# A block's attention in two unbroken stretches on TensorE, in place of up to six

## The chip, the cores and the metric

The kernel runs on one core of a Trainium2 chip. The metric is the device time of the whole program in microseconds (us). Times within the program come from one profiled execution, read by a hardware profiler.

## The reference

A linear attention with a complex decay for each channel runs over 768 tokens for 4 batches and 8 heads of 48 channels; its output goes through a two-layer network with a leaky ReLU.

```python
scale = np.minimum(mag, 0.999) / (mag + 1e-06)          # mag: of a_re + i a_im
for t in range(S):                                      # S = 768
    S_re, S_im = (ar*S_re - ai*S_im) + kv, ar*S_im + ai*S_re
    y[:, :, t] = np.einsum('bhd,bhde->bhe', q[:, :, t], S_re)
x = y.transpose(0, 2, 1, 3).reshape(3072, 384)
h = x @ w_in                                            # 384 -> 2048
return np.maximum(0.01 * h, h) @ w_out                  # 2048 -> 384
```

## The kernel before, in words

The 768 tokens of a batch are cut into six chunks of 128. A **block** is one chunk of one batch, all eight heads: 24 blocks. Two blocks make a **sub** `n` (0 to 11) and also a **group** `g` of 256 tokens for the network. (n, 0) and (n, 1) are the blocks of sub n. For each sub VectorE and ScalarE prepare decayed `q` and `k` (`prep`, L637: tiles `a`, `u`, `sq`, `xs`, `qk`, `qkt`), and twenty DMAs carry them from `qkt` into the layout by heads, `t96` (`relay_of`, L842; the trace writes `t`).

`attend` (L886) then does one block. On TensorE these are small matmuls of 32 columns of the array, and two sets of transposes of 128 columns:

- the **scores** of heads 0 to 3 and of heads 4 to 7, 16 matmuls each into a bank of PSUM; VectorE multiplies each half by the mask into `asb`;
- the **transposes** of `k` of heads 0 to 3 and 4 to 7, four each into a bank; ScalarE copies each to `kn`;
- the **output**, 32 matmuls (16 in the first chunk) of `asb` with `v` and of the state `rst` with `q`, into the bank `px`; ScalarE makes of it `x` rounded (`xh`), VectorE the rest (`xl`);
- the **update** of the state, 24 matmuls of `kn` with `v` into the bank `pu`; VectorE adds it to `rst`, ScalarE scales it eight times.

Blocks of the last chunk (subs 10 and 11) have neither transposes nor update. In the trace every small float32 matmul has two records, the transposes one to each. Attention has three PSUM banks (`att0` to `att2`, `NATT`, L33), handed out by `Banks` (L179).

`forward` (L1078) is the network on TensorE: for a group 16 pieces of `first` (`ph<-x`) and `second` (`po<-hid`), of 9, or of 6 wide matmuls of 256 columns, 288 wide matmuls in all; between them `hide` makes `hid` of `ph` (ScalarE `tg`, VectorE `tg`, ScalarE `hid`, VectorE `hid`).

The order on each engine is made by a planner when the program is built. `drive` (L218) keeps tasks; a task is a generator that stops with `yield "P"` (or `"V"`, `"A"`, `"S"`) ahead of its next instructions on that engine, with what it needs. The task that could start first goes on, and among those near it the one of the lowest rank: attention (`R_ATT`, -3) goes ahead of the network (`R_FF`, 1000). At each stop on TensorE the network can come in between. `Banks.done` says that a bank is free in the plan, and so at each stop `attend` asks for one. `PLACE` (L76) gives the places in a group's stream of the network from which on the blocks of the next sub may stand.

Of the kernel before, what the change touches and what calls it, by code (L numbers as in the profile page):

```python
# [7 lines left out]
F32 = mybir.dt.float32  # L8
# [5 lines left out]
AF = mybir.ActivationFunctionType  # L14
# [3 lines left out]
B, H, S, D = 4, 8, 768, 48  # L18
# [3 lines left out]
P = 128  # L22
C = 128
# [5 lines left out]
TI = 3  # L29
# [26 lines left out]
QKT, T96, X0, X1, V, A, KN, STG, ST, HID = (0, 1), (2, 3), 4, 5, 6, 7, 8, 9, 10, (11, 12, 13)  # L56
# [24 lines left out]
WSC = 2.0**20  # L81
# [3 lines left out]
def block_lane(h, x):  # L85
    return (x + h) % NB


def score_order():

    todo = [[(h, x) for h in range(NB) for x in range(NB) if block_lane(h, x) == q] for q in range(NB)]
    free = [0] * NB
    order = []
    while any(todo):
        q = min((f, q) for q, f in enumerate(free) if todo[q])[1]
        h, x = todo[q].pop(0)
        order.append((h, x))
        free[q] += NB - x
    return order


class Lane:


    def __init__(self, tc, engine, cost):
        self.tc, self.engine, self.cost = tc, engine, cost
        self.last, self.clock, self.log = None, 0.0, []
# [71 lines left out]
class Banks:  # L179
# [5 lines left out]
    @property  # L185
    def done(self):
        return bool(self.free)

    @property
    def end(self):  # L190
        return min(self.free)[0]

    def take(self):
        k = min(self.free)[1]
        self.free = [x for x in self.free if x[1] != k]
        return self.tiles[k]

    def give(self, tile, at):
        self.free.append((at, next(k for k, t in enumerate(self.tiles) if t is tile)))


class Task:
# [208 lines left out]
def body(ctx, tc, keep, a_in, qk_in, v_in, w_in, out):  # L411
# [3 lines left out]
    pp = ctx.enter_context(tc.tile_pool(name="pp", bufs=1))  # L415
# [14 lines left out]
    xacc = keep.tile([P, NT // C], F32, tag="xacc", name="xacc")  # L430
# [5 lines left out]
    pe, dve, act = Lane(tc, nc.tensor, pe_cost), Lane(tc, nc.vector, dve_cost), Lane(tc, nc.scalar, act_cost)  # L436
# [24 lines left out]
    banks = Banks(att)  # L461
# [43 lines left out]
    fetched_a, fetched_qk, fetched_v, prepared, moved_q, moved_k, attended, hidden, stored, checked = ({} for _ in range(10))  # L505
# [55 lines left out]
    def freed(*places):  # L561
        return [x for x, r in zip(converted, ROUND) if r in places]
# [310 lines left out]
    def from_block(t96, s, h, bi, x0, x1):  # L873
        t = t96[:, slot_of(s, h), bi, 0:C].rearrange("p (y x) -> p y x", x=NB)
        return t[:, :, x0] if x1 == x0 + 1 else t[:, :, x0:x1]
# [3 lines left out]
    def xgroup(u):  # L879
        g = u // NGU  # L880
        if g not in xg:
            x = pp.tile([P, 2, TI, GT], F32R, tag="x", name=f"x_{g}", bufs=2)
            xg[g] = [x[:, 0], x[:, 1]]
        return *xg[g], (u % NGU) * C

    def attend(n, bi):  # L886
        c, bs = SUBS[n]
        b = bs[bi]
        u = SUB_POS[n] // C + bi
        g = u // NGU  # L890
        carry = c < NCH - 1
        at = [[placed[n, 2 * bi + k]] if n > 1 else [] for k in range(2)]
        yield "P", moved_q[n], moved_k[n], banks, *at[0], *([over[u - 1]] if u else [masked])
        qkt, t96 = relay[n]
        am = []
        for hh in range(2):
            if hh:
                yield "+P", banks
            ps = banks.take()
            for h4, x in score_order():  # L900
                h = hh * 4 + h4
                q = block_lane(h4, x)
                mm(
                    ps[32 * q : 32 * q + 32, h4].rearrange("p (y x) -> p y x", x=NB)[:, :, x:],
                    lhsT=from_block(t96, 1, h, bi, x, x + 1),
                    rhs=from_block(t96, 0, h, bi, x, NB),
                    start=True,
                    stop=True,
                )
            yield "V"  # L910
            asb = pp.tile([P, 4, C], F32, tag="asb", name=f"asb_{n}_{bi}_{hh}", bufs=2)
            dve.tensor_tensor(out=asb, in0=ps, in1=mask, op=ALU.mult)
            am.append(asb)
            banks.give(ps, attended[u].end + 0.8)
        for hh in range(2 if carry else 0):
            yield "P" if hh else "+P", banks, *(at[1] if hh else []), *([] if u else freed(KN))
            if hh == 0:
                kn = pp.tile([P, H, 2, D], F32, tag="kn", name=f"kn_{n}_{bi}")
            pt = banks.take()
            for h4 in range(4):  # L920
                pe.transpose(
                    out=pt[:, h4, 0:96],
                    in_=t96[:, slot_of(1, hh * 4 + h4), bi, 0:C],
                    identity=ident[0:96, 0:96],
                )
            yield "A"
            act.copy(kn[:, hh * 4 : hh * 4 + 4].rearrange("p h l d -> p h (l d)"), pt[:, :, 0:96])
            banks.give(pt, attended[u].end + 0.6)

        yield "P", fetched_v[n], banks, *at[1], *(  # L930
            [summed[g - 2]] if g > 1 else freed((X0, X1)[g])
        )
        xh, xl, x0 = xgroup(u)
        v = raw_v[n]
        px = banks.take()
        lanes4 = [[] for _ in range(4)]
        for x in range(4 * TI):
            k, part = divmod(x, 3)
            for h, off in ([(2 * k, 0)], [(2 * k, 32), (2 * k + 1, 48)], [(2 * k + 1, 80)])[part]:
                cols = slice(k * PAIR + off, k * PAIR + off + 32)  # L940
                first = off != 48
                last = off != 32
                lanes4[x % 4].append((x // 4, v[:, bi, cols], am[h // 4][:, h % 4], first, last and c == 0))
                if c > 0:
                    lanes4[x % 4].append(
                        (x // 4, rst[:, b, k, off : off + 32], t96[:, slot_of(0, h), bi, 0:C], False, last)
                    )
        for step in zip(*lanes4):
            for q, (i, lhsT, rhs, first, last) in enumerate(step):
                mm(px[32 * q : 32 * q + 32, i], lhsT=lhsT, rhs=rhs, start=first, stop=last)  # L950
        yield "A"
        act.activation(
            xh[:, :, x0 : x0 + C], px[:, 0:TI], AF.Copy, scale=-WSC * WSC, accum_out=xacc[:, u : u + 1]
        )
        if carry:
            yield "+P", banks
            pu_bank = banks.take()
            pu = pu_bank.rearrange("p a b -> p (a b)")
            for h in range(H):
                o = VW + h * D  # L960
                for q in range(3):
                    mm(
                        pu[32 * q : 32 * q + 32, h * D : (h + 1) * D],
                        lhsT=kn[:, h].rearrange("p l d -> p (l d)")[:, 32 * q : 32 * q + 32],
                        rhs=v[:, bi, o : o + D],
                        start=True,
                        stop=True,
                    )
        over[u].set(attended[u].end + 1.0)
        yield "V"  # L970
        dve.scalar_tensor_tensor(
            out=xl[:, :, x0 : x0 + C], in0=px[:, 0:TI], scalar=-WSC * WSC, in1=xh[:, :, x0 : x0 + C].bitcast(F32),
            op0=ALU.mult, op1=ALU.subtract,
        )
        split[u].set(attended[u].end + 0.6)
        banks.give(px, attended[u].end + 0.6)
        if not carry:
            return
        new = pu[0:96, 0:DM].rearrange("p (k j e) -> p k j e", j=2, e=D)
        r0 = rst[:, b, 0, 0]  # L980
        r = bass.AP(r0.tensor, r0.offset, [list(r0.ap[0]), [PAIR, H // 2], [64, 2], [1, D]])
        if c > 0:
            yield "+V"
            dve.tensor_tensor(out=r, in0=new, in1=r, op=ALU.add)
            banks.give(pu_bank, attended[u].end + 0.6)
        yield "A"
        src = new if c == 0 else r
        for h0 in (0, 1, 6):
            hn = 2 if h0 == 6 else 3
            s0 = slot_of(1, h0)  # L990
            for x in range(hn):
                h = h0 + (x if h0 == 6 else 2 * x)
                act.activation(
                    r[:, h // 2, h % 2], src[:, h // 2, h % 2], AF.Copy, scale=t96[:, s0 + x, bi, C : C + 1]
                )
        if c == 0:
            banks.give(pu_bank, attended[u].end + 2.5)
# [106 lines left out]
    split, over = ([Mark() for _ in range(NT // C)] for _ in range(2))  # L1104
# [3 lines left out]
    masked = task(masks(), R_HID, end=4.5)  # L1108
# [101 lines left out]
```

## Time and profile before

| | us |
|---|---|
| median of three runs | 643.27 (642.04 to 644.84) |
| the profiled execution | 643.89 |
| its span, first to last instruction | 642.2 |
| TensorE busy | 602.5 (94%) |
| VectorE busy | 532.3 (83%) |
| ScalarE busy | 380.7 (59%) |

PE is TensorE, DVE VectorE, ACT ScalarE, SP the queue that issues the DMAs. The times of a matmul's end are modelled, since matmuls run into each other; so durations on TensorE are best taken from one start to the next. All lines of the trace that are recorded through the planner have the line L111; the tiles tell the instructions apart.

### The profile page before, as it was taken

The numbers are of one execution on the slowest core, as the hardware profiler recorded it, in microseconds if no ns is written. First come the engines' busy times: TensorE is split into PE (matmuls) and PEld (weight loads), VectorE is DVE, ScalarE is ACT, GpSimd is POOL, SyncE is SP. The second block draws the span as 40 slices with busy tenths as digits, with TensorE's granted clock in tenths as the row PEclk, the third lists the DMA queues.
The fourth block names the chain that finished last, engine by engine and source line by source line (L and its number), as shares of the span: only waits on it lengthen the run. The fifth ranks groups of instructions, "written<-read, shape, count | busy, mean of one in ns | idle before, by whom it ended". The sixth has DMA issues, their size and how long they took to land.

```text
span 642.2 us, 18140 instructions
## 1 busy us (share of the span) xinstructions
PE 602.5 (94%) x7714; PEld 554.4 (86%) x7714; DVE 532.3 (83%) x916; ACT 380.7 (59%) x838; POOL 10.3 (2%) x33
## 2 busy tenths in 40 slices
PE   4992899999979999999999999999999999999995
PEld 2451568999969999999999999999999999999994
DVE  6999899899899999998999999999898998342340
ACT  6975766475474574764755746636656637667631
POOL 2000100100000000000000000000000000000000
PEclk9995999999999999999999999999999999999998
DMA  8844621422423235045053153152260362877200
GB/s 344 317 137 123 239 79 51 150 80 78 123 80 98 102 96 169 17 131 146 4 150 128 31 138 111 61 150 69 85 175 21 102 200 85 255 214 269 99 1 30
DMA packets 30200, 79.25 MB, mean 123 GB/s; under 512 B 5120, under 2 KB 11264, under 8 KB 30112
## 3 DMA queue, kind: packets, MB, share of 16 engines
q1 hardware_dynamic: 29728, 77.23, 38.2%
q8 instruction: 62, 1.02, 0.6%
q0 software_dynamic: 384, 0.79, 0.5%
q14 instruction: 26, 0.21, 0.1%
HBM read 54.26 MB, written 4.72 MB: 92 GB/s over the span
## 4 chain that ended last, share of the span: by engine, by line
PE 67%; DVE 21%; DMA 3%; ACT 3%; issue 2%; SPq 1%; DVEq 0%; ACTq 0%
PE po L111 27%; PE ph L111 26%; PE att L111 13%; DVE qkt L111 4%; DVE a L111 4%; DMA a<-in_a_dram 3%; DVE u L111 3%; SPq L111 1%; DVE sq L111 1%; DVE hid L111 1%; DVE tg L111 1%; PE pd L111 1%; ACT sq L111 1%; DVE wcv L111 1%; DVE xs L111 1%
## 5 line engine op out<-in xcount | busy, mean ns | idle before, releaser
L111 PE MATMUL po<-hid,wout_hi 128*128 128x256 f32 x1152 | 231.1, 289 | 0.0
L111 PE MATMUL ph<-x,win_hi 128*128 128x256 f32 x1152 | 216.6, 286 | 3.7 <-DVE x L111 1.5
L111 PEld LDWEIGHTS po<-hid,wout_hi 128*128 128x128 f32 x1152 | 182.8, 188 | 7.0 <-issue 3.4
L111 PEld LDWEIGHTS ph<-x,win_hi 128*128 128x128 f32 x1152 | 178.8, 190 | 6.7 <-DVE x L111 2.0
L111 PE MATMUL ph<-x,win_lo 128*128 128x256 f32 x576 | 162.8, 283 | 0.0
L111 PE MATMUL po<-hid,wout_lo 128*128 128x256 f32 x576 | 142.9, 282 | 0.0
L111 PEld LDWEIGHTS ph<-x,win_lo 128*128 128x128 f32 x576 | 109.4, 190 | 0.0
L111 PEld LDWEIGHTS po<-hid,wout_lo 128*128 128x128 f32 x576 | 108.4, 188 | 0.0
L111 DVE TENSOR_TENSOR tg<-ph,tg 128x512 f32<-128x512 f32 x96 | 65.8, 686 | 39.1 <-ACT tg L111 38.6
L111 ACT ACTIVATE tg<-ph 128x512 f32<-128x512 f32 x96 | 56.9, 593 | 61.8 <-PE ph L111 61.5
L111 ACT CAST hid<-tg 128x512 fp32r<-128x512 f32 x96 | 59.1, 617 | 55.8 <-DVE tg L111 55.6
L111 DVE TENSOR_TENSOR hid<-tg,hid 128x512 fp32r<-128x512 f32 x96 | 65.8, 686 | 14.5 <-ACT hid L111 14.2
L111 DVE TENSOR_TENSOR u<-a 128x384 f32<-128x384 f32 x84 | 46.7, 556 | 3.1 <-ACT a L111 1.4
L111 DVE TENSOR_TENSOR qkt<-qk,a 128x768 f32<-128x768 f32 x48 | 44.7, 951 | 1.6 <-ACT qkt L111 1.6
L111 PE MATMUL att<-t 96*32 96x128 f32 (+3 forms) x1536 | 42.6, 253 | 2.7 <-DVE x L111 2.2
L111 DVE TENSOR_TENSOR asb<-att,mask 128x512 f32<-128x512 f32 x48 | 32.8, 689 | 13.2 <-PE att L111 12.7
L111 PEld LDWEIGHTS att<-t 96*32 96x32 f32 x1536 | 35.1, 144 | 9.4 <-DVE x L111 2.8
L111 PE MATMUL att<-asb,v 128*32 128x128 f32 x768 | 37.0, 275 | 1.2 <-DVE asb L111 0.9
L111 ACT ACTIVATE rst<-rst,t 96x48 f32<-96x48 f32 x128 | 30.7, 322 | 11.7 <-DVE rst L111 11.4
L111 ACT ACTIVATE wck<-wck 128x1152 f32<-128x1152 f32 (+1 forms) x22 | 27.7, 1259 | 9.0 <-DMA wck<-in_w_dram 8.8
L111 PE MATMUL att<-t,rst 96*32 96x128 f32 x640 | 32.3, 272 | 0.0
L111 DVE TENSOR_TENSOR a<-u 128x192 f32<-128x192 f32 x84 | 29.8, 354 | 1.5
(171 smaller groups left out, 767.7 us busy)
## 6 DMA issues: line engine op xcount, KB each, us to landing
t<-qkt SPq DMA_DIRECT2D x92, 145.1 KB, 3.3
wck<-in_w_dram SPq DMA_DIRECT2D x10, 1152.0 KB, 5.8
v<-in_v_dram SPq DMA_DIRECT2D x12, 832.0 KB, 5.9
a<-in_a_dram SPq DMA_DIRECT2D x12, 768.0 KB, 4.8
qk<-in_qk_dram SPq DMA_DIRECT2D x12, 768.0 KB, 6.5
out_dram<-ot SPq DMA_DIRECT2D x12, 384.0 KB, 5.5
t<-qkt SPq DMA_DIRECT2D x46, 64.5 KB, 3.0
stage_st<-in_w_dram SPq DMA_DIRECT2D x3, 768.0 KB, 9.5
```

The source lines that it names most:

```text
L111: x = getattr(self.engine, name)(*args, **kw)
```

## The change

For subs 1 to 11 (`once`) `attend` has two stops on TensorE instead of up to six. The first, taken when three banks are free in the plan (`banks.some(3)`), records both halves of the scores and the first transposes; the second, again with three free banks, records the second transposes, the output and the update. In the last chunk there are no transposes and update, and the stops ask for two banks and one. The masks stand together behind the first stretch on VectorE, and the first `kn` copy behind them on ScalarE. Sub 0 keeps its order. No instruction is added or taken away on any engine.

```diff
+    def some(self, n):
+        return Some(self, n)
+class Some:
+    def __init__(self, banks, n):
+        self.banks, self.n = banks, n
+    @property
+    def done(self):
+        return len(self.banks.free) >= self.n
+    @property
+    def end(self):
+        return sorted(self.banks.free)[self.n - 1][0]
...
-        yield "P", moved_q[n], moved_k[n], banks, *at[0], *([over[u - 1]] if u else [masked])
+        once = n > 0
+        yield "P", moved_q[n], moved_k[n], *at[0], *([over[u - 1]] if u else [masked]), (
+            banks.some((3 if carry else 2) if once else 1)
+        )
...
+        if once:
+            ps = [scores(0), scores(1)]
+            if carry:
+                kn = pp.tile([P, H, 2, D], F32, tag="kn", name=f"kn_{n}_{bi}")
+                pt = keys(0)
+            yield "V"
+            masked_out(0, ps[0])
+            yield "+V"
+            masked_out(1, ps[1])
+            if carry:
+                yield "+A"
+                natural(0, pt)
...
-        yield "P", fetched_v[n], banks, *at[1], *(
+        yield "P", fetched_v[n], banks.some((3 if carry else 1) if once else 1), *at[1], *(
             [summed[g - 2]] if g > 1 else freed((X0, X1)[g])
         )
+        if once and carry:
+            natural(1, keys(1))
...
+        if carry and once:
+            pu_bank, pu = update()
         yield "A"
         act.activation(
             xh[:, :, x0 : x0 + C], px[:, 0:TI], AF.Copy, scale=-WSC * WSC, accum_out=xacc[:, u : u + 1]
         )
-        if carry:
-            yield "+P", banks
+        if carry and not once:
+            yield "+P", banks
+            pu_bank, pu = update()
```

What it moves is shown at three places, all in block (7, 1). The first is on TensorE, at the end of the scores. `att_...<-t` are scores, `att_...<-ident,t` transposes, `po` and `ph` wide matmuls of the network. Before:

```order
L111 MATMUL att_103<-t_7_4816 32x32x2
L111 MATMUL att_103<-t_7_4816 32x32
L111 MATMUL po_0_4960<-hid_3_5031,wout_hi 128x256
L111 MATMUL po_0_4960<-hid_3_5031,wout_lo 128x256
L111 MATMUL po_1_4961<-hid_3_5031,wout_hi 128x256
L111 MATMUL po_1_4961<-hid_3_5031,wout_lo 128x256
L111 MATMUL po_2_4962<-hid_3_5031,wout_hi 128x256
L111 MATMUL po_2_4962<-hid_3_5031,wout_lo 128x256
L111 MATMUL att_102<-ident,t_7_4816 128x96 x4
```

After:

```order
L111 MATMUL att_103<-t_7_4835 32x32x2
L111 MATMUL att_103<-t_7_4835 32x32
L111 MATMUL att_101<-t_7_4835 32x128
L111 MATMUL att_101<-t_7_4835 32x32x3
...
L111 MATMUL att_101<-t_7_4835 32x32x2
L111 MATMUL att_101<-t_7_4835 32x32
L111 MATMUL att_102<-ident,t_7_4835 128x96 x4
L111 MATMUL po_0_4941<-hid_4_5062,wout_hi 128x256
```

The six wide matmuls ahead of the transposes are gone, and so are those between the halves: the second half (`att_101`) follows the first (`att_103`) and the transposes follow the second half.

The second place is on TensorE as well, from the output (`att<-asb,v` and `att<-t,rst`) to the update (`att<-v,kn`). Before:

```order
L111 MATMUL att_103<-asb_1_1_5301,v_4790 32x128 x4
L111 MATMUL att_103<-t_7_4816,rst 32x128 x4
L111 MATMUL po_0_4960<-hid_4_5128,wout_hi 128x256
L111 MATMUL po_0_4960<-hid_4_5128,wout_lo 128x256
L111 MATMUL po_1_4961<-hid_4_5128,wout_hi 128x256
L111 MATMUL po_1_4961<-hid_4_5128,wout_lo 128x256
L111 MATMUL po_2_4962<-hid_4_5128,wout_hi 128x256
L111 MATMUL po_2_4962<-hid_4_5128,wout_lo 128x256
L111 MATMUL att_102<-v_4790,kn_1_5303 32x48 x24
```

After:

```order
L111 MATMUL att_103<-ident,t_7_4835 128x96 x4
L111 MATMUL att_101<-asb_1_0_5334,v_4808 32x128 x4
...
L111 MATMUL att_101<-asb_1_1_5343,v_4808 32x128 x4
L111 MATMUL att_101<-t_7_4835,rst 32x128 x4
L111 MATMUL att_102<-v_4808,kn_1_5316 32x48 x24
L111 MATMUL ph_7_5353<-x_4499,win_hi 128x256 x2
```

Second transposes, output and update now stand in a row, with the network behind them.

The third place is VectorE, around the two masks (`asb`) of the block. Before:

```order
L111 TENSOR_TENSOR asb_1_0_5273<-att_101,mask 128x512
L111 TENSOR_TENSOR qkt_5130<-qk_5021,a_4321 128x6x128
L111 TENSOR_TENSOR asb_1_1_5301<-att_103,mask 128x512
L111 TENSOR_TENSOR tg_5_5275<-ph_5_5218,tg_5_5275 128x512
L111 TENSOR_TENSOR qkt_5130<-qk_5021,a_4321 128x6x128
```

After:

```order
L111 TENSOR_TENSOR qkt_5282<-a_4363 128x2x768
L111 TENSOR_TENSOR a_4363<-a_4363 128x1536
L111 TENSOR_TENSOR asb_1_0_5334<-att_103,mask 128x512
L111 TENSOR_TENSOR asb_1_1_5343<-att_101,mask 128x512
L111 TENSOR_TENSOR tg_6_5331<-ph_6_5251,tg_6_5331 128x512
```

The masks stand together, with two of the preparation's longest instructions ahead of them. Over the whole program the new order has, in all 18 full blocks of subs 1 to 9, 18 to 27 wide matmuls between the two stretches of a block, and 18 to 36 before the other block of the sub. In subs 5 to 9 the first block of a sub begins behind 189 wide matmuls of its group (138 to 162 before) and the second behind 234 (198 or 204 before).

## Rows read from the trace of the kernel before

**Rows 1.** The page, busy time of each engine.
```profile
PE 602.5 (94%) x7714; PEld 554.4 (86%) x7714; DVE 532.3 (83%) x916; ACT 380.7 (59%) x838; POOL 10.3 (2%) x33
```
**Rows 2.** Stretches: length, busy PE, PEld, DVE, ACT, POOL, PEclk, DMA share, GB/s.
```profile
104.00:233.26 129.26, 124.72 (x1790) 118.39 (x1788) 120.92 (x206) 74.53 (x177) 2.86 (x8) 0.99 0.31 94
233.26:509.61 276.35, 276.23 (x3942) 264.89 (x3937) 253.88 (x429) 163.51 (x387) 0.73 (x6) 1.00 0.35 101
...
233.26:279.21 45.95, 45.83 (x663) 44.07 (x658) 44.09 (x74) 30.02 (x73) 0.12 (x1) 1.00 0.39 119
```
**Rows 3.** Waits of TensorE from 100 us on: total us, times, longest.
```profile
PE ph L111 <- DVE x L111: 1.5, 1, 1.5
PE ph L111 <- ACT x L111: 1.1, 1, 1.1
```
**Rows 4.** TensorE in time, block (5, 1): start, length, instruction, count.
```profile
311.28 0.88 PE L111 MATMUL att<-t 96*32 96x128 f32 x32
312.09 0.98 PE L111 MATMUL po<-hid,wout_hi 128*128 128x256 f32 x6
312.91 0.49 PE L111 MATMUL att<-ident,t 96*128 96x96 f32 x4
313.19 0.49 PE L111 MATMUL ph<-x,win_hi 128*128 128x256 f32 x2
...
316.60 0.43 PE L111 MATMUL att<-asb,v 128*32 128x128 f32 x8
...
318.50 0.39 PE L111 MATMUL po<-hid,wout_hi 128*128 128x256 f32 x1
...
319.42 0.88 PE L111 MATMUL att<-v,kn 128*32 128x48 f32 x48
320.23 0.39 PE L111 MATMUL po<-hid,wout_hi 128*128 128x256 f32 x1
```
**Rows 5.** The chain that ended last, in time: start, length, what.
```profile
246.87 2.16 PE ph L111 x18
```
**Rows 6.** TensorE in time, block (4, 0).
```profile
254.71 1.52 PE L111 MATMUL att<-t 96*32 96x128 f32 x64
256.17 0.55 PE L111 MATMUL att<-ident,t 96*128 96x96 f32 x4
256.50 0.96 PE L111 MATMUL po<-hid,wout_hi 128*128 128x256 f32 x6
257.30 0.49 PE L111 MATMUL att<-ident,t 96*128 96x96 f32 x4
```
**Rows 7.** TensorE in time, block (2, 1): the output and the update.
```profile
184.41 0.43 PE L111 MATMUL att<-asb,v 128*32 128x128 f32 x8 [0.89 <-DVE asb L111]
...
186.19 0.86 PE L111 MATMUL att<-v,kn 128*32 128x48 f32 x48
```
**Rows 8.** VectorE in time, block (5, 1): in brackets idle time before, its releaser.
```profile
312.26 0.69 DVE L111 TENSOR_TENSOR asb<-att,mask 128x512 f32<-128x512 f32 x1 [0.18 <-PE att L111]
...
319.92 0.55 DVE L111 SCALAR_TENSOR_TENSOR x<-att,x 128x384 fp32r<-128x384 f32 x1
```
**Rows 9.** TensorE in time, block (2, 0): second scores, last of the output.
```profile
169.96 0.87 PE L111 MATMUL att<-t 96*32 96x128 f32 x32
...
175.51 0.41 PE L111 MATMUL att<-t,rst 96*32 96x128 f32 x8
```
**Rows 10.** VectorE in time, block (2, 0): second mask, and `x`.
```profile
173.19 0.68 DVE L111 TENSOR_TENSOR asb<-att,mask 128x512 f32<-128x512 f32 x1
...
180.48 0.55 DVE L111 SCALAR_TENSOR_TENSOR x<-att,x 128x384 fp32r<-128x384 f32 x1
```
**Rows 11.** The chain that ended last, up to the first wide matmuls of group 3.
```profile
209.18 4.69 DMA a<-in_a_dram
...
233.76 2.31 PE ph L111 x17
```
**Rows 12.** TensorE in time, block (1, 0): the rest of its second scores.
```profile
121.26 0.47 PE L111 MATMUL att<-t 96*32 96x128 f32 x10 [0.22 <-DMA t<-qkt]
```

More of the change, by code (lines that the diff above doesn't have):

```diff
@@ L892, in attend, with scores @@
         at = [[placed[n, 2 * bi + k]] if n > 1 else [] for k in range(2)]
-        yield "P", moved_q[n], moved_k[n], banks, *at[0], *([over[u - 1]] if u else [masked])
+        once = n > 0
+        yield "P", moved_q[n], moved_k[n], *at[0], *([over[u - 1]] if u else [masked]), (
+            banks.some((3 if carry else 2) if once else 1)
+        )
         qkt, t96 = relay[n]
         am = []
-        for hh in range(2):
-            if hh:
-                yield "+P", banks
+        kn = None
+        def scores(hh):
             ps = banks.take()
@@ L909, in attend, with masked_out @@
                 )
-            yield "V"
+            return ps
+        def masked_out(hh, ps):
             asb = pp.tile([P, 4, C], F32, tag="asb", name=f"asb_{n}_{bi}_{hh}", bufs=2)
@@ L914, in attend, with keys @@
             banks.give(ps, attended[u].end + 0.8)
[L915 to L918, printed above, removed]
+        def keys(hh):
             pt = banks.take()
@@ L925, in attend, with natural @@
                 )
-            yield "A"
+            return pt
+        def natural(hh, pt):
             act.copy(kn[:, hh * 4 : hh * 4 + 4].rearrange("p h l d -> p h (l d)"), pt[:, :, 0:96])
             banks.give(pt, attended[u].end + 0.6)
-        yield "P", fetched_v[n], banks, *at[1], *(
+        if once:
[10 more added lines that the diff above has]
+                natural(0, pt)
+        else:
+            for hh in range(2):
+                if hh:
+                    yield "+P", banks
+                ps = scores(hh)
+                yield "V"
+                masked_out(hh, ps)
+            for hh in range(2 if carry else 0):
+                yield "P" if hh else "+P", banks, *([] if u else freed(KN))
+                if hh == 0:
+                    kn = pp.tile([P, H, 2, D], F32, tag="kn", name=f"kn_{n}_{bi}")
+                pt = keys(hh)
+                yield "A"
+                natural(hh, pt)
+        yield "P", fetched_v[n], banks.some((3 if carry else 1) if once else 1), *at[1], *(
             [summed[g - 2]] if g > 1 else freed((X0, X1)[g])
         )
+        if once and carry:
+            natural(1, keys(1))
         xh, xl, x0 = xgroup(u)
@@ L950, in attend, with update @@
                 mm(px[32 * q : 32 * q + 32, i], lhsT=lhsT, rhs=rhs, start=first, stop=last)
[L951 to L954, printed above, removed]
-        if carry:
-            yield "+P", banks
+        def update():
             pu_bank = banks.take()
@@ L968, in attend @@
                     )
+            return pu_bank, pu
+        if carry and once:
+            pu_bank, pu = update()
+        yield "A"
+        act.activation(
+            xh[:, :, x0 : x0 + C], px[:, 0:TI], AF.Copy, scale=-WSC * WSC, accum_out=xacc[:, u : u + 1]
+        )
+        if carry and not once:
+            yield "+P", banks
+            pu_bank, pu = update()
         over[u].set(attended[u].end + 1.0)
```

## The prediction

> **What bounds the kernel now.** I read the page first, for the engines' shares, then the busy time by stretch, the waits of TensorE, the order of time on TensorE around single blocks, and last the same on VectorE. TensorE is busy 94% of the span [rows 1], but a share is no bound, so the stretches come next. From 233.26 to 509.61 us, six of the twelve groups, TensorE is busy 276.23 of 276.35 us at a granted clock of 1.00, and VectorE 253.88 us, 92% [rows 2]. The list of TensorE's waits from 100 us to the end has six entries, the two longest 1.5 and 1.1 us, for `x` [rows 3], and in time all of them lie before 234 us: behind that TensorE waits for nobody. So there each us that it spends less should shorten the kernel by one us, as long as nobody else becomes late. Before 233 us it is otherwise. The chain of waits comes there from a DMA of `a` through VectorE's preparation to the first matmul of a group [rows 11], with VectorE busy 120.92 of 129.26 us [rows 2].
>
> What does TensorE spend besides its matmuls? A wide matmul in an unbroken row costs 0.12 us (18 in 2.16 us) [rows 5]. Six of them are 0.72 us. In an ordinary block the six between the output and the update last from 318.50 to 319.42, 0.92 us [rows 4]: a visit of the small matmuls costs 0.20 us on the wide ones' side, half where they are left and half where they begin again. The six between the second scores and the transposes last 0.82 us, so going into transposes is free and only the leaving of the scores, 0.10 us, is paid. That is what the change works on: it moves instructions, and neither adds nor removes one.
>
> **The change, part by part.** Prices of one block, from starts in [rows 4], [rows 6] and [rows 7].
>
> Before, each stretch alone: a half of the scores 0.81 + 0.20 = 1.01, twice 2.02. Four transposes 0.28, and 0.08 at their exit (0.80 for the six behind transposes in [rows 6], against 0.72): 0.36, twice 0.72. The output 1.90 + 0.20 = 2.10. The update 0.81 + 0.20 = 1.01. Sum 5.85 us.
>
> After, first stretch: in block (4, 0) the halves of the scores already stand together, with the transposes behind them: 1.46 for both halves, 0.33 for the transposes, 0.08 for their exit and 0.10 for going in [rows 6]: 1.97. Second stretch: the output with the update straight behind it takes 1.78 in place of 1.90 (184.41 to 186.19) [rows 7], the update 0.81, the exit 0.10. What transposes with the output straight behind them cost no row shows without a wait. The bounds are 0.28 (nothing paid between them) and 0.46 (all that they pay today: 0.36, and the 0.10 for going into the output); I take 0.43, since the nearest row is the join of scores and transposes, which saved just 0.05. Sum 3.12. Together 5.09 us, 0.76 us less for a block (0.73 to 0.91 with the bounds).
>
> How many blocks: subs 0 to 11 have two blocks each. Sub 0 keeps its order. Subs 4 to 9, in the part bound by TensorE, are 12 blocks of full kind: 9.1 us. Some joins are there already: (4, 0) has both joins of its first stretch (0.36 + 0.05), and twice the next block's scores stand straight behind an update, once in sub 4 and once in sub 9, which the new order does not have (by the row of output and update about 0.32 each). That takes 1.05 off: 8.1 us. Subs 10 and 11 have no transposes and no update; their four blocks win the join of the scores alone, 2.02 - 1.46 - 0.20 = 0.36 each: 1.4 us. **Sum behind 233 us: 9.5 us.**
>
> Before 233 us (subs 1 to 3, six blocks) the same prices would give about 3.6 us net of joins that are there already. I count nothing: the chain there is VectorE's and the DMA's [rows 11], and a TensorE that comes sooner waits longer. Two places can get worse. The second half of sub 1's scores already waits for its relay until 121.26 [rows 12]; begun straight behind the first half it would wait about 1.5 us instead of 0.22. And in sub 3 the next group's `ph` now stands straight behind the update, where six wide matmuls covered 0.7 us of the wait for `x`. Bounds for this part: 1.5 us lost to 3.6 us won.
>
> New waits, and what covers them. The output needs both masks. VectorE gives the second mask 0.69 us after it starts, and in the part bound by TensorE it stands waiting for the scores: at 312.26 with 0.18 us of idle time, ended by TensorE [rows 8]. Now both masks come behind both halves, 0.6 to 1.3 us of work at the end of the scores; transposes (0.33), 15 to 27 wide matmuls (1.8 to 3.2 us) and, in full blocks, transposes again (0.4) lie before the output, so this costs nothing. The update needs the second `kn` copy, which ScalarE, busy 163.51 of 276.35 us [rows 2], has 1.78 us of the output to make. The scores of the next block need the banks of `px` and `pu`: VectorE's `x` starts at 319.92, 1.42 us behind the first wide matmul after the output [rows 4, 8], and the cover is the update (0.81), 18 or 24 wide matmuls (2.2 or 2.9) and half of the scores. Behind the scores, the transposes and the output stand in VectorE's and ScalarE's queues `tg` and `hid` of the forward pass; the order leaves 18 wide matmuls or more between stretches, so that these have a stage's time. Nothing here is late if VectorE keeps up, and that is the first rival.
>
> On [rows 6] a rule of the Trainium skill can be weighed. The page "TensorEngine Tiling (Array Packing)", section Key Properties, says that changing the tiling mode, not just the tile, drains TensorE. The transposes use all 128 columns, as the wide matmuls do, and the other small ones 32, so by the rule a join with transposes would save nothing and the joins of scores with scores and output with update all. That agrees with the 0.05 us that the row shows for scores and transposes, and would make 0.68 of the 0.76 us and the sum 8.6 us.
>
> The profiled execution took 643.89 us (span 642.2 and 1.7 around it), 0.62 above the median of 643.27. Less 9.5 us it would be 634.4; on the median's scale 633.8.
>
> **The rivals.** *VectorE becomes the bound.* Subs 4 to 9 would run in 276.35 - 8.1 = 268.2 us, and VectorE's 253.88 us would be 95% of it; in the densest group it has 44.09 of 45.95 us, 96% [rows 2]. For it: preparation runs its long instructions between the masks, with waits for ScalarE among them. Against it: some of its idle time is waiting for TensorE itself [rows 8], and 96% occurs. If it holds at about 94%, the six groups take 270 us, and with some waits of TensorE half of the 8.1 us goes: 636 to 640, 638 as its time.
>
> *The banks make it slower.* There are three banks for attention, and each stretch of a full block needs all three, so scores cannot begin before the `x` of the block before has left its bank. Where VectorE is full this is long: in sub 2 the second scores start at 169.96 and their mask only at 173.19; the last eight records of the output start at 175.51 and its `x` at 180.48 [rows 9, 10], about 5 us. The cover above is about 4 us up to that bank, and about 2.9 us for the masks. So if masks and `x` come as late as in sub 2 everywhere, TensorE waits about 1.0 us for the bank and 0.3 us for the masks in each of 18 blocks, 23 us, against 9.5 won: 657. From 0.53 us of waits in a block the gain is gone. Against it: the masks of [rows 8] start with TensorE, not behind it. The Trainium skill, page "Perfetto Trace Analysis", section Optimizing Tensor Performance, wants independent groups of matmuls to rotate through PSUM banks so that evacuation overlaps; taking all three at once speaks against the change in just this way, and no row of a stretch that does so can confirm it.
>
> *The early part gains too*, all 3.6 us: 630.2. Against it stands its chain [rows 11].
>
> *It does not do what it says.* The planner could have torn the stretches apart again; but in the new order a full block has two stretches in all 18 changed cases, so little is left of this one: 643.
>
> **How the numbers follow.** Forecast (632 to 636.5) 0.56; VectorE the bound (636.5 to 641) 0.18; early gain (below 632) 0.12; the banks 0.08; no effect 0.06. The likeliest gives 633.8. The range goes down to 630, where the early gain ends, and up to 640, the slower end of VectorE's case, leaving about 0.15 outside. A measurement of this kernel can tell some 0.5%, 3.2 us, from no change: faster means below 640.05, slower above 646.5. Forecast, early gain and most of VectorE's case are faster, 0.85; no effect, and small cases of the banks and of VectorE, 0.09; slower 0.06.
>
> **What the profile would show.** Right: from about 233 us TensorE still without waits, a group of 288 wide matmuls and two blocks in about 44.6 us instead of 46.1, scores of 1.46 us followed by transposes, output and update in one piece of 2.6 us. Wrong: waits of TensorE for `asb`, `x` or `rst` at the head of the stretches (banks), or for `x` and the relays at group starts with VectorE above 95% (VectorE). If a block saves clearly other than 0.76 us, it is the join of transposes and output that I priced wrongly; if groups are 1.5 us shorter and the total is not about 9.5 less, the start of the part bound by TensorE has moved later than 233 us.

## The result, and the profile after

| | before | after |
|---|---|---|
| median | 644.0 us (4 runs) | 635.25 us (4 runs) |
| ratio | 1 | 0.9867 (95% interval 0.9835 to 0.9899) |
| profiled execution | 643.89 us | 636.34 us |
| its span | 642.2 us | 634.6 us |

The changed kernel is 1.3% faster. The forecast was 633.8 us with a range of 630 to 640.

TensorE first, in time, around the same block as [rows 4], block (5, 1): start, length, instruction, count.

```profile
313.21 1.53 PE L111 MATMUL att<-t 96*32 96x128 f32 x64
314.67 0.55 PE L111 MATMUL att<-ident,t 96*128 96x96 f32 x4
315.00 0.36 PE L111 MATMUL po<-hid,wout_hi 128*128 128x256 f32 x1
...
318.32 0.50 PE L111 MATMUL att<-ident,t 96*128 96x96 f32 x4
318.75 0.42 PE L111 MATMUL att<-asb,v 128*32 128x128 f32 x8
...
320.54 0.86 PE L111 MATMUL att<-v,kn 128*32 128x48 f32 x48
321.33 0.50 PE L111 MATMUL ph<-x,win_hi 128*128 128x256 f32 x2
```

Both halves of the scores take 1.46 us, the transposes 0.33; after 27 wide matmuls come the second transposes (0.43), output (1.79) and update (0.79). No wide matmul stands within a stretch, and no wait.

Next the stretches of the changed kernel, cut where a group's first `ph` begins: length, busy PE, PEld, DVE, ACT, POOL, PEclk, DMA share, GB/s. The rows answer to [rows 2].

```profile
231.61:279.97 48.36, 47.72 (x656) 46.72 (x657) 42.61 (x73) 26.74 (x66) 0.12 (x1) 0.93 0.30 94
279.97:324.67 44.70, 44.70 (x658) 43.90 (x657) 41.61 (x71) 27.14 (x67) 0.12 (x1) 1.00 0.35 112
324.67:503.39 178.72, 178.72 (x2626) 175.49 (x2625) 164.52 (x281) 105.77 (x253) 0.48 (x4) 1.00 0.32 100
```

From 279.97 us on a group takes 44.7 us (178.72 for four), TensorE is busy all of it at full clock, and VectorE is 92% busy. Before, it was 276.35 us for six groups, 46.1 each, and 46.13 for a group in which no stretches stood together already:

```profile
325.37:371.50 46.13, 46.13 (x659) 44.19 (x657) 43.24 (x75) 26.54 (x67) 0.12 (x1) 1.00 0.33 97
```

But the group from 231.61 us takes 48.36 us, more than before (45.95), and its granted clock is 0.93. The waits of TensorE after 100 us (total, times, longest) say why; they answer to [rows 3]:

```profile
PE ph L111 <- ACT x L111: 3.3, 2, 2.1
PE att L111 <- DVE asb L111: 1.3, 1, 1.3
PE ph L111 <- DVE x L111: 1.3, 2, 0.6
PE att L111 <- DMA t<-qkt: 0.9, 1, 0.9
PE att L111 <- ACT wout_hi L111: 0.4, 1, 0.4
```

And in time, at the start of group 3:

```profile
228.63 0.86 PE L111 MATMUL att<-v,kn 128*32 128x48 f32 x48
231.61 0.39 PE L111 MATMUL ph<-x,win_hi 128*128 128x256 f32 x1 [2.13 <-ACT x L111]
232.64 0.58 PE L111 MATMUL ph<-x,win_hi 128*128 128x256 f32 x1 [0.64 <-DVE x L111]
233.02 0.41 PE L111 MATMUL ph<-x,win_lo 128*128 128x256 f32 x1
233.23 0.63 PE L111 MATMUL ph<-x,win_hi 128*128 128x256 f32 x2
233.66 0.41 PE L111 MATMUL ph<-x,win_lo 128*128 128x256 f32 x1
...
238.56 0.38 PE L111 MATMUL po<-hid,wout_hi 128*128 128x256 f32 x1
238.78 0.28 PE L111 MATMUL po<-hid,wout_lo 128*128 128x256 f32 x1
```

TensorE stands 2.13 and 0.64 us waiting for `x` of block (3, 1). Behind it a wide matmul takes 0.21 us instead of 0.12 (three from 233.02 to 233.66) until 238.78. The granted clock is at its lower level there, 1.2 GHz:

```profile
232.00:236.00 4.00, 3.36 (x15) 3.36 (x16) 2.78 (x5) 2.65 (x9) 0.00 (x0) 0.50 0.31 129
```

The 28 wide matmuls from 232.64 on took 6.14 us; at 0.12 they are 3.36, so the low clock cost 2.8 us, as much as the two waits together. The waits come from the queues of ScalarE and VectorE, which both have the next preparation ahead of `x`. ScalarE, then VectorE, in time:

```profile
227.74 0.48 ACT L111 COPY kn<-att 128x384 f32<-128x384 f32 x1
229.61 1.49 ACT L111 ACTIVATE qkt<-a 128x1536 f32<-128x1536 f32 x1 [1.39 <-DVE a L111]
231.00 0.47 ACT L111 ACTIVATE x<-att 128x384 fp32r<-128x384 f32 x1
```

```profile
230.30 1.82 DVE L111 TENSOR_TENSOR qkt<-qk,a 128x768 f32<-128x768 f32 x2
232.04 0.55 DVE L111 SCALAR_TENSOR_TENSOR x<-att,x 128x384 fp32r<-128x384 f32 x1
```

The output is done at about 228.8 us, and ScalarE is idle until 229.61. But the square of the preparation stands ahead of `x` in its queue, waits for VectorE's `a`, and then takes 1.4 us. That ends the first wait. The second ends with VectorE's part of `x`, which starts only at 232.04, behind preparation that keeps VectorE busy without a pause from 225 us on. In this order VectorE would have held TensorE until 232.64 even with ScalarE's part ready earlier.

Before, the same place looked like this, TensorE and VectorE:

```profile
232.45 0.88 PE L111 MATMUL att<-v,kn 128*32 128x48 f32 x48
233.26 0.89 PE L111 MATMUL ph<-x,win_hi 128*128 128x256 f32 x2
```

```profile
233.16 0.55 DVE L111 SCALAR_TENSOR_TENSOR x<-att,x 128x384 fp32r<-128x384 f32 x1
```

In the changed kernel's execution the update begins 3.8 us sooner (228.63 against 232.45), and VectorE's `x` only 1.1 us sooner (232.04 against 233.16). The difference is the wait.

So the account between the two profiled executions is this. Up to the first `ph` of group 3 1.65 us are won (233.26 against 231.61); in group 3 2.41 are lost (45.95 against 48.36); from group 4 on 8.4 are won (642.2 - 279.21 = 363.0 against 634.6 - 279.97 = 354.6). The first of the three is not shown to be the change's: the version below that keeps the old order up to here begins group 3 at 231.09 us in one execution and at 233.40 in another.

### The profile page after: what moved, and what is told of

Read it like the earlier page. It is cut to its first block, busy times and chain, and to the rows that moved or that the text cites. A ratio compares the mean times of both kernels' runs of the same rounds, so it can differ in the third digit from the quotient of the medians.

```text
span 634.6 us, 18137 instructions
## 1 busy us (share of the span) xinstructions
PE 593.1 (93%) x7714; PEld 554.4 (87%) x7714; DVE 531.2 (84%) x916; ACT 378.6 (60%) x838; POOL 10.2 (2%) x33
## 4 chain that ended last, share of the span: by engine, by line
PE 64%; DVE 23%; DMA 5%; ACT 4%; issue 2%; SPq 0%; DVEq 0%; ACTq 0%
PE ph L111 26%; PE po L111 26%; PE att L111 11%; DMA a<-in_a_dram 4%; DVE qkt L111 4%; DVE a L111 4%; DVE u L111 3%; DVE hid L111 2%; PE pd L111 2%; DVE sq L111 2%; DVE tg L111 1%; DVE xs L111 1%; DVE asb L111 1%; ACT sq L111 1%; DVE wcv L111 1%
## 5 line engine op out<-in xcount | busy, mean ns | idle before, releaser
L111 PE MATMUL po<-hid,wout_hi 128*128 128x256 f32 x1152 | 224.8, 284 | 0.0
L111 PEld LDWEIGHTS ph<-x,win_hi 128*128 128x128 f32 x1152 | 180.7, 191 | 7.9 <-ACT x L111 3.5
L111 DVE TENSOR_TENSOR qkt<-qk,a 128x768 f32<-128x768 f32 x48 | 45.1, 952 | 3.9 <-ACT qkt L111 3.7
L111 PE MATMUL att<-t 96*32 96x96 f32 (+3 forms) x1536 | 38.0, 251 | 2.5 <-DMA t<-qkt 0.9
L111 PEld LDWEIGHTS att<-t 96*32 96x32 f32 x1536 | 33.7, 144 | 6.7 <-issue 1.5
L111 ACT COPY kn<-att 128x384 f32<-128x384 f32 x40 | 18.9, 476 | 27.5 <-PE att L111 23.0
L111 DVE TENSOR_TENSOR asb<-att,mask 128x512 f32<-128x512 f32 x48 | 31.0, 683 | 1.1 <-PE att L111 0.9
```

The source lines that it names most:

```text
L111: x = getattr(self.engine, name)(*args, **kw)
```

## The experiments

Two claims are to be told apart from their rivals: that the gain is the price of joins (two stretches of small matmuls with no wide matmul between them), each kind with its own price; and that what is missing from it lies at group 3, in a wait for `x` and the low clock behind it.

**The old order for subs 1 to 3.**

```diff
-        once = n > 0
+        once = n > 3
```

> Subs 1 to 3 keep the old order, subs 4 to 11 have the two stretches. Theory (waits and the clock): group 3 is long in the changed kernel (231.61 to 279.97, 48.36 us) because TensorE waited 2.1 and 0.6 us for x of block (3, 1) and its clock was then granted at half speed until 238.77. With the old order of sub 3, six wide matmuls and the update cover that wait as before (one wait of some 0.5 us), the clock stays, group 3 takes 45.95 less the joins of sub 4, 0.8, so 45.2 us, and the rest from group 4 on 354.6 us as in the changed kernel: span 233.3 + 45.2 + 354.6 = 633.1 us. Rival (VectorE is late in group 3 because the attention of sub 4 stands later in its group): group 3 stays near 48 us without a low clock, span about 636.

Measured: 634.72 us, 0.9855 of before (0.9827 to 0.9883); span 631.0. Its stretches, cut at the starts of groups 3, 4 and 5:

```profile
231.09:276.63 45.54, 45.03 (x662) 44.03 (x657) 41.33 (x72) 28.57 (x73) 0.12 (x1) 1.00 0.38 118
276.63:321.30 44.67, 44.67 (x658) 43.88 (x657) 41.59 (x72) 27.43 (x65) 0.12 (x1) 1.00 0.37 106
```

and its only wait of TensorE after 225 us:

```profile
PE ph L111 <- DVE x L111: 0.5, 1, 0.5
```

Group 3 is 45.54 us at full clock, 2.8 us shorter than in the changed kernel, and the later groups are the same 44.67. The span is 2.1 us below the expected 633.1, since group 3 begins 2.2 us earlier than the 233.3 taken from the kernel before. The rival's 48 us did not come: the later attention is not what makes group 3 long. From group 3 to the end it takes 399.9 us against 408.9 before: 9.1 us won.

**Only subs 1 to 3 in two stretches.**

```diff
-        once = n > 0
+        once = 0 < n < 4
```

> Only subs 1 to 3 have the two stretches, subs 4 to 11 the old order. Theory: up to group 3 as in the changed kernel (231.6 us), group 3 again long by the wait for x and half the clock (about 49 us, since sub 4 has the old stretches), then about 362.5 us as before, a little less for three joins that the planner makes by itself: span about 643. So the early part of the change gives nothing or costs 1 us. Rival (the early blocks gain their 3.6 us and group 3 is long for a reason in the later part): span about 639.

Measured: 646.6 us, 1.0049 of before (1.0023 to 1.0075), slower; span 643.1. Group 3 and group 4:

```profile
231.01:279.27 48.26, 47.59 (x657) 45.69 (x657) 42.49 (x72) 26.64 (x63) 0.12 (x1) 0.96 0.28 90
279.27:327.22 47.95, 46.51 (x657) 44.34 (x657) 44.29 (x74) 29.33 (x72) 0.12 (x1) 1.00 0.36 108
```

Group 3 is long again, with clock 0.96, and group 4 has another wait for `x` of 1.4 us. The rival's gain of 3.6 us in the early blocks did not come. The early part of the change by itself costs 3 us (1.5 to 4.8 by the interval; 0.9 us in the profiled execution); a part of that is the wait in group 4, which the full change does not have.

**The wait at group 3 covered.** In the stream of group 3 the two pieces left of group 2 go first:

```diff
-        order = [(first, g, 0), *late, (first, g, 1), (first, g, 2)]
+        order = [*late, (first, g, 0), (first, g, 1), (first, g, 2)] if g == 3 else [(first, g, 0), *late, (first, g, 1), (first, g, 2)]
```

> The changed kernel, with one thing moved: at the start of group 3 the two second pieces that are left of group 2 (36 wide matmuls, 4.3 us) stand ahead of the first ph of group 3, not behind it. Theory: the wait for x of block (3, 1), 2.1 + 0.6 us, is covered, the clock is not lowered behind it (30 matmuls of 0.21 in place of 0.12 us, 2.9 us), and both are won: span 634.6 - 5.6 = 629.0, up to 631.5 if VectorE, full there, gives a part of it back as waits. Rival (VectorE or the preparation paces this part): the waits move behind group 3's start, span 633 or more.

Measured: 634.3 us, 0.985 (0.9818 to 0.9881); span 631.7. Cut at the starts of groups 3 to 6 (group 3's now lies 36 wide matmuls later in the row):

```profile
234.17:274.52 40.35, 40.35 (x622) 39.56 (x621) 35.80 (x65) 24.21 (x60) 0.12 (x1) 1.00 0.31 98
274.52:320.39 45.87, 44.94 (x658) 43.85 (x656) 43.81 (x74) 27.98 (x64) 0.12 (x1) 1.00 0.31 98
320.39:366.75 46.36, 45.06 (x656) 44.04 (x657) 42.86 (x74) 27.67 (x65) 0.12 (x1) 1.00 0.36 112
366.75:411.40 44.65, 44.65 (x658) 43.87 (x657) 42.30 (x73) 28.60 (x75) 0.12 (x1) 1.00 0.38 111
```

The wait at group 3 is gone, the clock stays at 1.00, and group 4 starts at 274.52 us instead of 279.97: 5.45 us, against 5.6 expected. Then half of it goes: groups 4 and 5 take 45.87 and 46.36 us, with 0.9 and 1.3 us of waits for VectorE's `x`, VectorE 96% busy in the first of them. At the end 2.9 us are left (a span of 631.7 against 634.6). Both theories had a part. Wait and clock explain group 3, and behind it waits for VectorE take about half of that back. In the medians this kernel and the changed one can't be told apart.

**The transposes at stops of their own**, scores in one stretch, output and update in another:

```diff
-        once = n > 0
+        js, jt, ju = n > 0, False, n > 0
         yield "P", moved_q[n], moved_k[n], *at[0], *([over[u - 1]] if u else [masked]), (
-            banks.some((3 if carry else 2) if once else 1)
+            banks.some(1 + js + (js and jt and carry))
         )
...
-        if once and carry:
+        if jt and carry:
             natural(1, keys(1))
...
-        if carry and once:
+        if carry and ju:
             pu_bank, pu = update()
```

`js` joins the halves of the scores, `jt` puts the transposes into the two stretches, `ju` joins output and update; without `jt` the transposes stand behind the masks at two stops, as in the kernel before.

> The changed kernel, but the transposes stand at stops of their own as before, with wide matmuls around them: scores in one stretch, each set of transposes alone, output and update in one stretch. Theory (a join with transposes saves next to nothing, 0.05 and 0.03 us; the joins of scores with scores and of output with update 0.36 and 0.32): a group from 5 to 8 takes 44.68 + 2 x 0.08 = 44.85 us. Rival (each visit to the small matmuls costs the same, 0.2 us and the exit): two visits more for a block, at least 44.68 + 4 x 0.2 = 45.5 us. In the order 24 wide matmuls stand between the update of block (3, 1) and the first ph of group 3, so the wait there and the half clock behind it should be gone: span about 634.6 + 1.0 - 4 = 631.5 by the theory of waits and clock, 635.5 without it.

Measured: 635.62 us, 0.9857 (0.9827 to 0.9887). Groups 4 and 5:

```profile
279.93:324.73 44.80, 44.80 (x659) 43.97 (x658) 41.01 (x70) 26.46 (x64) 0.12 (x1) 1.00 0.35 103
324.73:369.53 44.80, 44.80 (x658) 43.96 (x657) 43.79 (x76) 28.81 (x70) 0.12 (x1) 1.00 0.30 98
```

44.80 against 44.68 us: taking the transposes out, two visits more for each of two blocks, costs 0.12 us a group, 0.06 us a block (0.08 expected). The rival, an equal price for each visit, wanted 0.8. The rule of the Trainium skill that the prediction weighed (page "TensorEngine Tiling (Array Packing)", section Key Properties) says that a change of tiling mode drains TensorE. The transposes use 128 columns in the trace, as the wide matmuls do, so by that reading their own stops should cost nothing; the trace agrees with it here to within that 0.06 us.

The wait at group 3 did not vanish as expected: 0.8 us were left, without a low clock behind it. Group 3 itself is shorter, 45.86 us (234.07 to 279.93) against 48.36. But the span of 635.4 us is what the expectation gave for the case that wait and clock explain nothing, not its 631.5. The difference lies ahead of group 3, which begins 2.5 us later than in the changed kernel; 1.8 us of that are there already at 105.08 us, where the changed kernel stands at 103.27. So the total of this run does not bear out the expectation; only the length of group 3 does.

**The join of the scores alone**, then **the join of output and update alone**, by the same three names:

```diff
-        js, jt, ju = n > 0, False, n > 0
+        js, jt, ju = n > 0, False, False
```

```diff
-        js, jt, ju = n > 0, False, n > 0
+        js, jt, ju = False, False, n > 0
```

> Only the halves of the scores are joined, in subs 1 to 11; transposes, output and update stand alone as before. Theory (the prices of the rows): in the part without waits a group takes 46.13 - 2 x 0.36 = 45.4 us, the groups with the last chunk 42.0 as in the changed kernel. Rival (the cost is that of the number of visits alone, 1.43 us for a group's eight joins of the changed kernel): two joins of eight save 0.36, 45.8 us.

Measured in one run: 640.86 us. Groups 5 and 6:

```profile
325.22:370.67 45.45, 45.45 (x659) 43.93 (x657) 41.13 (x70) 26.38 (x63) 0.12 (x1) 1.00 0.37 114
370.67:416.13 45.46, 45.46 (x659) 43.96 (x657) 41.33 (x71) 28.02 (x67) 0.12 (x1) 1.00 0.33 100
```

> Only output and update are joined, in subs 1 to 9; scores and transposes stand as before. Theory (prices): a group takes 46.13 - 2 x 0.32 = 45.5 us where the planner joins nothing else, and 0.41 less, 45.1 us, where it joins scores and transposes by itself (first blocks of subs 6, 7 and 9 in the order). Rival (number of visits alone): 45.8 us. The groups with the last chunk 42.75 as before, or 42.4 where two halves of scores stand together.

Measured in one run: 638.26 us. Group 5, where the planner had joined the next sub's first scores and transposes by itself, and group 7, where it had not:

```profile
323.36:368.48 45.12, 45.12 (x659) 44.04 (x657) 40.77 (x72) 27.93 (x68) 0.12 (x1) 1.00 0.35 105
413.60:459.11 45.51, 45.51 (x658) 44.20 (x657) 40.64 (x72) 25.62 (x61) 0.12 (x1) 1.00 0.32 95
```

Both fit the prices: 45.46 where 45.4 was expected and 45.8 by the rival; 45.51 and 45.12 where 45.5 and 45.1 were. Against 46.13 the scores give 0.67 us a group and output with update 0.62; with the 0.12 of the transposes that is 1.41, and the whole change gives 1.45. The single times (640.86 and 638.26) stand the other way round to the prices; one run each can't rank them. Up to group 3 they differ by 1.7 us on their own (234.04 and 232.34 us), and the second has the joins that the planner made by itself.

**Both versions again on one chip**, the changed kernel and the one with the old order for subs 1 to 3.

> The changed kernel once more, on one chip with the next: 635.3 us, 0.987 of before. A group from 5 to 8 takes 44.68 us; a wait of about 2.8 us for x at group 3, behind which the clock is lowered.

> The old order for subs 1 to 3 and the two stretches from sub 4 on, once more. Theory (the stretches of subs 1 to 3 gain nothing and cost a wait and low clock at group 3): 1 to 3 us faster than the changed kernel, 0.983 to 0.986 of before, and from group 3 on 399.9 us against 402.9. Rival (the low clock comes and goes from run to run in both alike): no difference between the two.

Measured: 636.74 us, 0.9884 (0.9855 to 0.9914), and 634.37 us, 0.9852 (0.9824 to 0.9880). Group 3 in the one and in the other:

```profile
231.91:279.04 47.13, 46.49 (x656) 45.47 (x657) 42.44 (x73) 26.67 (x66) 0.12 (x1) 0.96 0.31 96
```

```profile
233.40:278.90 45.50, 45.00 (x663) 44.02 (x657) 41.32 (x72) 28.48 (x72) 0.12 (x1) 1.00 0.39 118
```

From group 3 to the end 401.8 against 400.2 us. The intervals overlap: the medians favour the old early order, by 2.4 us here and by 0.5 in the earlier runs, but do not prove it. In the traces the loss at group 3 is there each time in the one and never in the other; that is two executions of each.

## Why the prediction was right, point by point

*The bound.* TensorE was busy without a wait from 233 us on, and each us taken from it there came off the end: groups 4 to 8 took 44.7 us as forecast (about 44.6), and VectorE, 92% busy in the shorter groups, did not become the bound. The first rival fell, though not by much: where TensorE comes 5 us earlier at group 4, as in the third experiment, it waits for VectorE.

*The prices.* Scores joined 1.46 and 0.33 with transposes, as in [rows 6]; output and update 1.79 and 0.79 (1.78 and 0.81). The one price without a row, transposes with the output straight behind, was taken as 0.43 between 0.28 and 0.46 and measured 0.43. The sum behind 233 us was 9.5; without the trouble at group 3 it is 9.1 and 8.8 us (399.9 and 400.2 against 408.9). 0.4 us of the difference is the wait of 0.5 us that is left there, against 0.1 before. What takes the 0.3 us between 9.1 and 8.8 stays open.

*The banks.* The slower rival did not come in the part bound by TensorE. VectorE's `x` begins at 321.63 in block (5, 1), 0.3 us after the update, and the next scores come at 347.44. The tighter place is between the two blocks of a sub: there `x` of (5, 0) is done at 310.8 us, and the scores of (5, 1) begin at 313.21. VectorE in time:

```profile
310.21 0.56 DVE L111 SCALAR_TENSOR_TENSOR x<-att,x 128x384 fp32r<-128x384 f32 x1 [0.19 <-ACT x L111]
...
314.60 1.28 DVE L111 TENSOR_TENSOR asb<-att,mask 128x512 f32<-128x512 f32 x2
...
321.63 0.55 DVE L111 SCALAR_TENSOR_TENSOR x<-att,x 128x384 fp32r<-128x384 f32 x1
```

Both masks end at 315.9, the output that needs them begins at 318.75. In sub 2, where [rows 9, 10] showed late masks, a wait for the masks did come once: 1.3 us for `asb` (the list of waits above).

*The step that was mis-sized* is that of sub 3 in the early part: "six wide matmuls covered 0.7 us of the wait for `x`". It was right that the wait would grow there, and in the bound of 1.5 us lost for the part it stood too small. The wait grew from 0.12 us (45.95 less 45.83 busy, [rows 2]) to 2.77, because preparation stood ahead of `x` in both queues. Most of that is TensorE coming sooner, which the prediction had said would only wait. What it had no term for is the clock: the low clock behind the wait cost 2.8 us in the profiled execution. The comparison with the old early order shows it by itself: 0.64 us of the wait lie in group 3, where that version waits 0.5, and still the group is 2.8 us longer. So of the 9.1 us 3.1 went, and 6.0 were left (8.4 won behind group 3, 2.4 lost in it). The prediction had named this sign: groups 1.5 us shorter and a total short of 9.5 would mean that the part bound by TensorE starts later than 233 us. At full clock and without waits it started at 238.78.

The same loss is smaller in another execution (group 3 of 47.13 us in place of 48.36). The start up to group 3, counted at nothing, was 1.65 us earlier in the profiled execution, so the forecast missed by 1.9 us on the profiled execution's scale and 1.45 on the median's. That it came so near is in part luck: the start varies by as much between executions of one program, and without it the miss is 3.5 us.

*Sub 1* is not settled: its second scores waited 0.9 us for the relay in the first execution of the changed kernel and 0.22 in the second, where the prediction had about 1.5; before it was 0.22 [rows 12].

## What to carry to other kernels

Where one engine is busy without waits, price its order from starts: the difference between six matmuls in a row and six between two visits was the whole gain, and it held in each partial version to within 0.05 us a group. Which neighbours share an order matters more than how many visits there are: here scores with scores and output with update gave nine tenths, the transposes one. And where an edit is made for a bound stretch, apply it there: in the stretch before, bound by other engines, the cover that it took away (the wide matmuls that ran while `x` was made) turned into a wait, and in all three profiled executions with that wait of 2 us a low clock stood behind it.

## What was not expected of the hardware

The low clock does not follow a wait of a given length. Before, TensorE waited 0.89, 1.14 and 1.51 us at the start of group 2 [rows 3, 7], and had a low clock between 188 and 200 us; in both profiled executions of the version with the old early order it waited the same, 0.9, 1.1 and 1.5 us, and the clock stayed. The stretch from 188 to 200 us, before and in the first execution of that version:

```profile
188.00:200.00 12.00, 10.30 (x71) 10.10 (x72) 11.56 (x15) 8.12 (x22) 0.00 (x0) 0.86 0.50 138
```

```profile
188.00:200.00 12.00, 10.90 (x88) 10.70 (x89) 11.94 (x18) 8.22 (x22) 0.00 (x0) 1.00 0.40 119
```

Likewise the waits of 2.1 and 0.6 us at group 3 were followed by a low clock that left 0.93 over group 3 in one execution of the changed kernel and 0.96 in the other, 1.2 us apart in length. The version with two stretches in subs 1 to 3 alone waited 1.14 and 0.65 us at the start of group 2 and kept a clock of 1.00 from 188 to 192 us; the changed kernel waited 1.14 and 0.64 there and had 0.63. What decides between them no run here shows. A difference of 1.2 us between two executions of one program is half of the 2.4 us that the last comparison tried to measure.
